# A top-k attention and gated feed-forward kernel: padded value tails, joined q and k tails, and a new order inside the slot

## The chip, the core and the metric

The kernel runs on one core of a Trainium2 chip. The metric is the time of one execution on the device in microseconds (us). PE is TensorE (PEld its weight loads), DVE is VectorE, ACT is ScalarE, POOL is GpSimd, SP is the queue that issues all DMAs of this kernel.

## What is computed

```python
batch, n_heads, seq, head_dim = (8, 8, 576, 64)          # q, k, v in float32
scores = scale * np.matmul(q, k.transpose(0, 1, 3, 2))
kth = np.partition(scores, -32, axis=-1)[..., -32:-31]
scores = np.where(scores >= kth, scores, -1e9)
scores = scores - np.max(scores, axis=-1, keepdims=True)
attn = np.exp(scores)
attn = attn / (np.sum(attn, axis=-1, keepdims=True) + 1e-09)
x = np.matmul(attn, v)                 # then (B,H,S,D) -> (B*S, H*D) = (4608, 512)
h = x @ w_in                           # w_in (512, 2048)
g = h * (1.0 / (1.0 + np.exp(-1.702 * h)))
out = g @ w_out                        # w_out (2048, 512)
```

## The kernel before

A row of 576 positions is four full tiles of 128 (`FULL` = 512) and a tail of 64 (`TAIL`). Heads are taken in pairs, four pairs a batch. The program is a list of 144 slots, 18 for each of the 8 batches: 16 slots of one query tile and one pair of heads, and two tail slots, in which the 64 last queries of two pairs share the 128 rows. Slot n works on several stages at once: the top-32 search on the scores of n (`topk`), the exponentials of n-1, the transposed weights and the product with v of n-2 (`turn`, `turn_tail`, `values`), the scores of n+1, and one quarter of a feed-forward tile (`hidden`: 16 matmuls of 128 columns into `ph`; `tanh`; `gate`; and, one slot later, `project`: 4 matmuls of 512 columns into `po`). A float32 matmul stands as two in the trace. A feed-forward tile is begun when the values of its four pairs are there; its fourth `project` is followed by `ob`, the copy of the result on ScalarE.

All engines run in the order in which the program is written. On TensorE a slot is: `turn`, `hidden`, `turn_tail`, `project`, `prepare` where there is one, `scores`, `values`. On ScalarE: the two copies of `turn`, the exponentials, the copy of `turn_tail`, tanh, the two preparatory operations on weights (`round_piece`), `ob`, the copies of `prepare`, the two copies of the scores, the copy of the values. VectorE does `topk` as a chain of 14 operations, with `divide` (two small ones; GpSimd then scales the weights `pr`) behind the ninth and `gate` behind the tenth.

`prepare` transposes one q or k tile pair: four full transposes and one of the 64 tail rows, each into a buffer of `ps_t`, which has two; `turn`, `turn_tail` and the output `o` of `values` use the same two. The tail of k is written at both ends of `k_t`, so that the scores of head 0 end with the tail keys and those of head 1 begin with them, and the two tails lie side by side in `pr`. The tail of v (`v_t`) is loaded twice, once for each half of the partitions, and `values` multiplies it from 64 partitions.

The weights, 32 pieces of 128x512, come in as 64-bit numbers and are rounded in the first slots, three a slot: `cut` and `sign` on VectorE (L137, L142), an addition on GpSimd (L146) and `normal` on VectorE (L149), with two temporaries from ScalarE (`more` L133, `size` L134) out of a pool of two buffers each.

Of the kernel before, what the change touches and what calls it, by code (L numbers as in the profile page):

```python
# [16 lines left out]
P = 128  # L17
# [9 lines left out]
def kernel(  # L27
# [44 lines left out]
    assert D == 64 and 2 * TAIL == P and C == NP * P and C == PIECE and HALF <= 512 and B % 2 == 0  # L72
# [5 lines left out]
    temps = pool("temps", 2)  # L78
# [78 lines left out]
    loaded = {}  # L157

    def load(name, b, hp):
        src = q if name == "q" else k  # L160
        t = loaded[name, b, hp] = loads.tile([P, NF + 1, 2, D], F32, name=f"{name}_l")
        for j in range(2):
            nc.sync.dma_start(
                t[:, 0:NF, j, :], src[b, 2 * hp + j, 0:FULL, :].rearrange("(t p) d -> p t d", p=P)
            )
        nc.sync.dma_start(
            t[0:TAIL, NF, :, :], src[b, 2 * hp : 2 * hp + 2, FULL:S, :].rearrange("h p d -> p h d")
        )

    def load_v(b, hp):  # L170
# [6 lines left out]
        tail = vals.tile([P, 2, D], F32, name="v_t")  # L177
        for i in range(2):
            nc.sync.dma_start(
                tail[i * TAIL : (i + 1) * TAIL, :, :],  # L180
                v[b, 2 * hp : 2 * hp + 2, FULL:S, :].rearrange("h p d -> p h d"),
            )
        vv[b, hp] = main, tail

    def prepare(name, b, hp):
# [5 lines left out]
        scale = SCALE if name == "q" else 1.0  # L191
        full = ps_t.tile([P, 512], F32, name="tp")
        for t in range(NF):
            nc.tensor.transpose(full[:, t * P : (t + 1) * P], src[:, t, :, :], ident[:])  # L194
        nc.scalar.mul(out=dst[:, before : before + FULL], in_=full[:], mul=scale)  # L195
# [15 lines left out]
    def scores(n):  # L211
        b, t, hps = slots[n]
        ps = [ps_s.tile([P, 2, 512], F32, name="s_ps") for _ in range(2)]
        if t < NF:
            parts = [(j, j, slice(0, P), slice(t * P, (t + 1) * P)) for j in range(2)]
        else:
            parts = [(i, j, slice(j * TAIL, (j + 1) * TAIL), slice(FULL, S)) for i in range(2) for j in range(2)]
        for c in range(2):
            for i, j, rows, cols in parts:
                on = slice(j * D, (j + 1) * D)  # L220
                nc.tensor.matmul(  # L221
                    ps[i][rows, c, 0:HALF],
                    lhsT=qT[b, hps[i]][on, cols],
                    rhs=kT[b, hps[i]][on, FIRST[i] + c * HALF : FIRST[i] + (c + 1) * HALF],
                )
# [56 lines left out]
    def turn(n):  # L282
        pr = st[n]["pr"]
        pt = st[n]["pt"] = ptp.tile([P, 2 * NF + 1, P], F32, name="pt")
        for i in range(2):
            tp = ps_t.tile([P, 512], F32, name="tp")
            for c in range(NF):
                nc.tensor.transpose(tp[:, c * P : (c + 1) * P], pr[:, MAIN[i] + c * P : MAIN[i] + (c + 1) * P], ident[:])  # L288
            nc.scalar.copy(out=pt[:, i * NF : (i + 1) * NF, :].rearrange("p c r -> p (c r)"), in_=tp[:])  # L289

    def turn_tail(n):

        tp = ps_t.tile([P, 512], F32, name="tp")
        nc.tensor.transpose(tp[:, 0:P], st[n]["pr"][:, FULL : FULL + P], ident[:])  # L294
        nc.scalar.copy(out=st[n]["pt"][:, 2 * NF, :], in_=tp[:, 0:P])
# [3 lines left out]
    def values(n):  # L299
# [3 lines left out]
        if t < NF:  # L303
            groups = [(0, [(j, slice(0, P), j) for j in range(2)])]
        else:
# [199 lines left out]
```

## Time and profile before

| | |
|---|---|
| Time, median of 3 runs | 1758.56 us (1758.18 to 1758.82) |
| Time of the profiled execution | 1759.57 us |
| Its span, first to last instruction | 1757.8 us |
| PE busy | 1640.2 us (93%) |
| DVE busy | 1582.3 us (90%) |
| ACT busy | 993.6 us (57%) |
| POOL busy | 599.1 us (34%) |
| Mean granted TensorE clock | 0.972 of full speed |

The busy share is a mean over two very different stretches: in the first 200 us the weights are rounded, and behind them all slots are alike. Each is read by itself.

### The profile page before, as it was taken

What the parts mean: (1) busy time and instruction counts of PE and PEld (TensorE: products, weight loads), DVE (VectorE), ACT (ScalarE), POOL (GpSimd) and SP (SyncE); (2) the same over time, 40 slices, a digit from 0 to 9 for tenths busy, and PEclk for the clock granted to TensorE, in tenths of its full rate; (3) what the DMA queues carried; (4) which work ended last, traced back from release to release, by engine and by line L of the source; (5) the groups of instructions that cost most, each with busy time, mean ns of one, the idle gap of its engine ahead of it and who ended that gap; (6) DMA issues with size and microseconds to landing.
All of it is one profiled execution on the core that took longest, in us unless ns stands there. A gap on an engine that the chain in (4) does not pass through costs nothing.

```text
span 1757.8 us, 31495 instructions
## 1 busy us (share of the span) xinstructions
PE 1640.2 (93%) x11856; PEld 1176.6 (67%) x11856; DVE 1582.3 (90%) x3408; ACT 993.6 (57%) x2149; POOL 599.1 (34%) x614
## 2 busy tenths in 40 slices
PE   2446899999999999999999999999999999999998
PEld 1225677667777777777777776777777777777776
DVE  5899998999899998999989998999989998999940
ACT  3456556656555555556565565555565565555530
POOL 2455432333333333333333333333323333333320
PEclk9668999999999999999999999999999999999999
DMA  7234001101000101010010100110010100000000
GB/s 198 77 112 123 12 16 36 37 6 28 21 22 21 35 21 35 14 35 22 20 29 21 35 21 21 29 35 22 19 30 21 35 21 20 22 7 7 7 7 13
DMA packets 129815, 57.61 MB, mean 33 GB/s; under 512 B 120960, under 2 KB 120960, under 8 KB 129664
## 3 DMA queue, kind: packets, MB, share of 16 engines
q1 hardware_dynamic: 129664, 55.60, 12.0%
q8 instruction: 94, 1.54, 0.4%
q14 instruction: 57, 0.47, 0.1%
HBM read 46.14 MB, written 9.44 MB: 32 GB/s over the span
## 4 chain that ended last, share of the span: by engine, by line
PE 87%; DVE 8%; ACT 1%; issue 1%; POOL 1%; SPq 1%; DMA 0%; POOLq 0%; DVEq 0%
PE ph L353 28%; PE po L391 27%; PE o L318 11%; PE s_ps L221 10%; PE tp L288 8%; DVE top L237 3%; DVE left L240 2%; PE tp L194 2%; PE tp L294 1%; DVE win L142 1%; ACT k_t L195 1%; DVE win L137 1%; DVE wout L142 1%; POOL pr L280 0%; PE tp L197 0%
## 5 line engine op out<-in xcount | busy, mean ns | idle before, releaser
L280 POOL TENSOR_SCALAR pr<-pr,rden 128x576 f32<-128x576 f32 x288 | 493.4, 1725 | 924.7 <-DVE rden L277 801.1
L237 DVE MAX8 top<-left 128x8 f32<-128x576 f32 x864 | 623.0, 747 | 0.0
L391 PE MATMUL po<-wout,gT 128*128 128x512 f32 x1152 | 518.0, 592 | 0.0
L353 PE MATMUL ph<-xT,win 128*128 128x128 f32 x4096 | 483.9, 277 | 0.0
L353 PEld LDWEIGHTS ph<-xT,win 128*128 128x128 f32 x4096 | 473.4, 194 | 0.5 <-issue 0.5
L240 DVE MATCH_REPLACE8 left<-top,left 128x576 f32<-128x576 f32 x576 | 423.4, 743 | 0.0
L391 PEld LDWEIGHTS po<-wout,gT 128*128 128x128 f32 x1152 | 207.8, 190 | 207.1 <-issue 206.8
L228 ACT COPY sc<-s_ps 128x576 f32<-128x576 f32 x288 | 169.8, 642 | 304.5 <-PE s_ps L221 304.5
L237 DVE MAX8 top<-sc 128x8 f32<-128x576 f32 x288 | 204.5, 751 | 104.9 <-ACT sc L228 101.4
L288 PE MATMUL tp<-ident,pr 128*128 128x128 f32 x1152 | 172.7, 289 | 53.8 <-POOL pr L280 37.8
L267 ACT ACTIVATE pr<-sc,low 128x576 f32<-128x576 f32 x288 | 219.3, 764 | 0.0
L240 DVE MATCH_REPLACE8 left<-top,sc 128x576 f32<-128x576 f32 x288 | 211.9, 743 | 0.0
L265 ACT ACTIVATE sc<-sc,cut 128x576 f32<-128x576 f32 x288 | 207.5, 771 | 0.0
L221 PE MATMUL s_ps<-k_t,q_t 64*128 64x288 f32 (+1 forms) x1280 | 202.8, 436 | 1.6 <-ACT k_t L195 1.6
L289 ACT COPY pt<-tp 128x512 f32<-128x512 f32 x288 | 157.5, 586 | 52.8 <-PE tp L288 52.6
L288 PEld LDWEIGHTS tp<-ident,pr 128*128 128x128 f32 x1152 | 124.4, 144 | 91.5 <-POOL pr L280 41.1
L221 PEld LDWEIGHTS s_ps<-k_t,q_t 64*128 64x128 f32 (+1 forms) x1280 | 114.6, 183 | 93.5 <-issue 71.1
L318 PEld LDWEIGHTS o<-pt,v_l 128*64 128x64 f32 x2560 | 129.2, 138 | 59.9 <-issue 41.2
L318 PE MATMUL o<-pt,v_l 128*64 128x128 f32 (+1 forms) x2560 | 165.0, 272 | 0.0
L377 DVE SCALAR_TENSOR_TENSOR gT<-th,ph 128x512 f32<-128x512 f32 x144 | 96.5, 670 | 49.5 <-ACT th L370 49.5
L370 ACT ACTIVATE th<-ph 128x512 f32<-128x512 f32 x144 | 86.8, 603 | 32.2 <-PE ph L353 32.2
L396 ACT ACTIVATE ob<-po 128x512 f32<-128x512 f32 x36 | 21.5, 598 | 97.6 <-PE po L391 97.6
(45 smaller groups left out, 905.7 us busy)
## 6 DMA issues: line engine op xcount, KB each, us to landing
v_l<-in_v_dram SPq DMA_DIRECT2D x64, 128.0 KB, 2.5
q_l<-in_q_dram SPq DMA_DIRECT2D x64, 128.0 KB, 2.5
k_l<-in_k_dram SPq DMA_DIRECT2D x64, 128.0 KB, 2.5
raw<-in_moe_w_in_dram SPq DMA_DIRECT2D x16, 512.0 KB, 4.8
raw<-in_moe_w_out_dram SPq DMA_DIRECT2D x16, 512.0 KB, 3.8
out_dram<-ob SPq DMA_DIRECT2D x32, 256.0 KB, 2.1
v_t<-in_v_dram SPq DMA_DIRECT2D x64, 32.0 KB, 2.2
q_l<-in_q_dram SPq DMA_DIRECT2D x32, 32.0 KB, 2.3
```

The lines of the kernel that those rows point to most:

```text
L221: nc.tensor.matmul(ps[i][rows, c, 0:HALF], lhsT=qT[b, hps[i]][on, cols], rhs=kT[b, hps[i]][on, FIRST[i] + c * HALF : FIRST[i] + (c + 1) * ...
L228: nc.scalar.copy(out=sc[:, i, :].rearrange("p (c k) -> p c k", c=2), in_=ps[i][:, :, 0:HALF])
L237: nc.vector.max(top[:, i, 8 * r : 8 * r + 8], (left if r else sc)[:, i, :])
L240: nc.vector.match_replace(left[:, i, :], top[:, i, 8 * r : 8 * r + 8], (left if r else sc)[:, i, :], LOWEST)
L265: nc.scalar.activation(sc[:, i, :], sc[:, i, :], AF.Prelu, bias=cut[:, i : i + 1], alpha=HUGE)
L267: nc.scalar.activation(pr[:, i * S : (i + 1) * S], sc[:, i, :], AF.Exp, bias=low[:, i : i + 1], accum_out=den[:, i : i + 1],)
L280: nc.gpsimd.tensor_scalar(on, on, rden[:, i : i + 1], None, op0=ALU.mult)
L288: nc.tensor.transpose(tp[:, c * P : (c + 1) * P], pr[:, MAIN[i] + c * P : MAIN[i] + (c + 1) * P], ident[:])
L289: nc.scalar.copy(out=pt[:, i * NF : (i + 1) * NF, :].rearrange("p c r -> p (c r)"), in_=tp[:])
L318: nc.tensor.matmul(dst, lhsT=lhsT, rhs=rhs, start=(c == 0), stop=(c == NF))
L353: nc.tensor.matmul(ph[:, i, :], lhsT=win[:, c, f * P : (f + 1) * P], rhs=xT[:, c, :], start=(c == 0), stop=(c == CC - 1),)
L391: nc.tensor.matmul(po[:], lhsT=gT[:, i, :], rhs=wout[:, f, :], start=(f == 0), stop=(f == FC - 1))
```

## The change

Six edits, made together. (1) The tail of v lies in one of six constant tiles `v_e`, zero but for head 0's tail in the upper left and head 1's in the lower right quarter, and `values` multiplies it from all 128 partitions, as it does the full tiles. (2) The tails of q and k of a pair come into one tile `ends` and are turned by one transpose, in the `prepare` of k. (3) In tail slots the two score tiles are now the two heads, and the rows the two pairs (before, the other way round); the four quarter-size products go in the order (0,0), (1,1), (0,1), (1,0) of row half and column half. (4) The order inside the slot: `scores` and `values` come before `project`, `prepare` before them, the exponentials before the copies of `turn`; `divide` stands behind the sixth operation of the chain and `gate` behind the last; `hidden` starts as soon as a tile is ready (slot 6, before slot 7). (5) Three buffers for each temporary of the weights, whose ScalarE operations now stand at the end of the slot ahead. (6) Two pieces are loaded and rounded ahead of the first chain, and the loads of q and k stand ahead of those of v.

```diff
-    temps = pool("temps", 2)
+    temps = pool("temps", 3)
...
+    v_ends = [const.tile([P, 2, D], F32, name=f"v_e{i}") for i in range(6)]
+    for t in v_ends:
+        nc.gpsimd.memset(t[:], 0.0)
...
-        tail = vals.tile([P, 2, D], F32, name="v_t")
-        for i in range(2):
-            nc.sync.dma_start(
-                tail[i * TAIL : (i + 1) * TAIL, :, :],
-                v[b, 2 * hp : 2 * hp + 2, FULL:S, :].rearrange("h p d -> p h d"),
-            )
+        tail = v_ends[(b * NP + hp) % len(v_ends)]
+        for j in range(2):
+            nc.sync.dma_start(tail[j * TAIL : (j + 1) * TAIL, j, :], v[b, 2 * hp + j, FULL:S, :])
...
-        tail = ps_t.tile([P, 512], F32, name="tp")
-        nc.tensor.transpose(tail[:, 0:TAIL], src[0:TAIL, NF, :, :], ident[0:TAIL, 0:TAIL])
-        for left_at in (0, before + FULL) if before else (FULL,):
-            nc.scalar.mul(out=dst[:, left_at : left_at + TAIL], in_=tail[:, 0:TAIL], mul=scale)
+        if name == "k":
+            ends = ps_t.tile([P, 512], F32, name="tp")
+            nc.tensor.transpose(ends[:, 0:P], loaded.pop(("ends", b, hp))[:], ident[:])
+            nc.scalar.mul(out=qT[b, hp][:, FULL:S], in_=ends[:, 0:TAIL], mul=SCALE)
+            for to in (0, before + FULL):
+                nc.scalar.copy(out=dst[:, to : to + TAIL], in_=ends[:, TAIL:P])
...
-            parts = [(j, j, slice(0, P), slice(t * P, (t + 1) * P)) for j in range(2)]
+            parts = [(i, 0, slice(0, P), slice(t * P, (t + 1) * P)) for i in range(2)]
         else:
-            parts = [(i, j, slice(j * TAIL, (j + 1) * TAIL), slice(FULL, S)) for i in range(2) for j in range(2)]
+            parts = [(i, p, slice(p * TAIL, (p + 1) * TAIL), slice(FULL, S)) for i, p in ((0, 0), (1, 1), (0, 1), (1, 0))]
...
-                    if c < NF:
-                        lhsT, rhs = main[:, c, j, :], pt[:, tile_ * NF + c, cols]
-                    else:
-                        on = slice(half * TAIL, (half + 1) * TAIL)
-                        lhsT, rhs = tail[on, j, :], pt[on, 2 * NF, cols]
-                    nc.tensor.matmul(dst, lhsT=lhsT, rhs=rhs, start=(c == 0), stop=(c == NF))
+                    nc.tensor.matmul(
+                        o[j * D : (j + 1) * D, 0 : cols.stop - cols.start],
+                        lhsT=main[:, c, j, :] if c < NF else tail[:, j, :],
+                        rhs=pt[:, j * NF + c if c < NF else 2 * NF, cols],
...
-        if 0 <= n - 2 < N:
-            turn(n - 2)
-        if n >= NPIECE // RATE - NG + 1:
-            hidden()
         if 0 <= n - 1 < N:
             bounds(n - 1)
             exponentials(n - 1)
         if 0 <= n - 2 < N:
-            turn_tail(n - 2)
-        tanh()
-        rounding = [round_piece(x) for x in by_slot[n]] if 0 <= n < len(by_slot) else []
-        project()
+            turn_main(n - 2)
+        hidden()
+        if 0 <= n - 2 < N:
+            turn_ends(n - 2)
         for fn, args in todo:
             if fn is prepare:
                 fn(*args)
+        tanh()
         if n + 1 < N:
             scores(n + 1)
         if 0 <= n - 2 < N:
             values(n - 2)
+        project()
+        if n == -1:
+            begin_rounding(-1)
+        begin_rounding(n + 1)
...
-            if i == 8 and 0 <= n - 1 < N:
+            if i == 5 and 0 <= n - 1 < N:
                 divide(n - 1)
-            if i == 9:
-                gate()
...
+        gate()
```

On TensorE an ordinary slot, from the transposes of `pr` on, stood thus before:

```order
L288 MATMUL tp<-ident,pr 128x128 x8
L353 MATMUL ph<-xT,win 128x128 x16
L294 MATMUL tp<-ident,pr 128x128
L391 MATMUL po<-wout,gT 128x512 x4
L221 MATMUL s_ps<-k_t,q_t 128x288 x4
L318 MATMUL o<-pt,v_l 64x128 x8
L318 MATMUL o<-pt,v_t 64x128 x2
```

The same slot of the changed kernel, where `v_e_126` is one of the six tail tiles:

```order
L297 MATMUL tp<-ident,pr 128x128 x8
L361 MATMUL ph<-xT,win 128x128 x16
L297 MATMUL tp<-ident,pr 128x128
L229 MATMUL s_ps<-k_t,q_t 128x288 x4
L320 MATMUL o<-pt,v_l 64x128 x8
L320 MATMUL o<-pt,v_e_126 64x128 x2
L399 MATMUL po<-wout,gT 128x512 x4
```

The four wide matmuls of `project` moved from ahead of the scores to the end of the slot, and the transposes of the next slot now follow them.

On ScalarE the part of a slot around `ob`, the copy of a finished feed-forward tile, stood thus before (from tanh to the exponentials of the next slot):

```order
L370 ACTIVATE th<-ph 128x512
L396 ACTIVATE ob<-po 128x512
L228 COPY sc<-s_ps 128x576 x2
L324 COPY xT<-o 128x128
L289 COPY pt<-tp 128x512 x2
L265 ACTIVATE sc<-sc,cut 128x576 x2
L267 ACTIVATE pr,den<-sc,low 128x576 x2
```

And in the changed kernel:

```order
L378 ACTIVATE th<-ph 128x512
L236 COPY sc<-s_ps 128x576 x2
L332 COPY xT<-o 128x128
L404 ACTIVATE ob<-po 128x512
L273 ACTIVATE sc<-sc,cut 128x576 x2
L275 ACTIVATE pr,den<-sc,low 128x576 x2
L298 COPY pt<-tp 128x512 x2
```

`ob` moved behind the copies of scores and values, directly ahead of the exponentials, and the two copies of `turn` moved behind these.

On VectorE the program began with the first chain:

```order
L237 MAX top<-sc 128x8 x2
L137 TENSOR_SCALAR win<-raw 128x512
L240 MATCH_REPLACE left<-top,sc 128x576
L142 SCALAR_TENSOR_TENSOR win<-raw,win 128x512
L240 MATCH_REPLACE left<-top,sc 128x576
```

It now begins with two whole pieces of weights:

```order
L137 TENSOR_SCALAR win<-raw 128x512
L142 SCALAR_TENSOR_TENSOR win<-raw,win 128x512
L137 TENSOR_SCALAR win<-raw 128x512
L142 SCALAR_TENSOR_TENSOR win<-raw,win 128x512
L149 SCALAR_TENSOR_TENSOR win<-size,win 128x512 x2
L245 MAX top<-sc 128x8 x2
```

All six operations on the first two pieces, the two `normal` included, stand ahead of the first search.

## Rows read from the trace of the kernel before

**Rows 1.** Windows: length; busy PE, PEld, DVE, ACT, POOL; clock, DMA share, GB/s

```profile
200.00:1700.00 1500.00, 1489.19 (x10974) 1069.91 (x10973) 1404.75 (x3060) 884.36 (x1926) 509.55 (x534) 1.00 0.09 23
```

**Rows 2.** Waits of PE and of DVE from 200 to 1700: us, times, longest

```profile
PE tp L194 <- ACT k_t L195: 6.9, 14, 0.5
...
DVE top L237 <- ACT sc L228: 75.9, 116, 2.5
```

**Rows 3.** Timeline of PE, an ordinary slot: start us, us, what

```profile
600.93 0.43 PE L318 MATMUL o<-pt,v_t 64*64 64x128 f32 x4
601.29 1.16 PE L288 MATMUL tp<-ident,pr 128*128 128x128 f32 x8
602.29 3.74 PE L353 MATMUL ph<-xT,win 128*128 128x128 f32 x32
...
605.97 3.60 PE L391 MATMUL po<-wout,gT 128*128 128x512 f32 x8
609.50 1.24 PE L221 MATMUL s_ps<-k_t,q_t 64*128 64x288 f32 x8
610.67 1.09 PE L318 MATMUL o<-pt,v_l 128*64 128x128 f32 x16
611.69 0.43 PE L318 MATMUL o<-pt,v_t 64*64 64x128 f32 x4
```

**Rows 4.** Timeline of PE, tail slots: values of one, scores of another

```profile
704.71 0.69 PE L318 MATMUL o<-pt,v_l 128*64 128x64 f32 x16
705.33 0.33 PE L318 MATMUL o<-pt,v_t 64*64 64x64 f32 x4
...
706.47 1.10 PE L288 MATMUL tp<-ident,pr 128*128 128x128 f32 x8
...
855.62 2.16 PE L221 MATMUL s_ps<-k_t,q_t 64*64 64x288 f32 x16
857.71 1.09 PE L318 MATMUL o<-pt,v_l 128*64 128x128 f32 x16
```

**Rows 5.** Timeline of DVE: the starts of four chains that waited for nothing

```profile
89.45 1.41 DVE L237 MAX8 top<-sc 128x8 f32<-128x576 f32 x2
105.16 1.41 DVE L237 MAX8 top<-sc 128x8 f32<-128x576 f32 x2
...
209.48 1.40 DVE L237 MAX8 top<-sc 128x8 f32<-128x576 f32 x2
219.99 1.41 DVE L237 MAX8 top<-sc 128x8 f32<-128x576 f32 x2
```

**Rows 6.** Timeline of ACT: the exponentials of a slot, first and last, and one `ob`

```profile
602.97 1.44 ACT L265 ACTIVATE sc<-sc,cut 128x576 f32<-128x576 f32 x2
...
605.74 0.19 ACT L267 ACTIVATION_READ_ACCUMULATOR pr<-sc,low 128x1 f32 x1
...
620.37 0.60 ACT L396 ACTIVATE ob<-po 128x512 f32<-128x512 f32 x1 [2.67 <-PE po L391]
```

**Rows 7.** Timeline of the start: DMA issues on SP, two ACT operations on weights

```profile
0.71 1.00 SPq L173 DMA_DIRECT2D v_l<-in_v_dram  x2
...
3.21 1.15 SPq L163 DMA_DIRECT2D q_l<-in_q_dram  x2
...
10.56 1.54 SPq L115 DMA_DIRECT2D raw<-in_moe_w_in_dram  x3
...
15.81 0.67 ACT L133 ACTIVATE more<-raw 128x512 int32<-128x512 uint32 x1 [2.30 <-DMA raw<-in_moe_w_in_dram]
...
28.35 0.66 ACT L134 ACTIVATE size<-raw 128x512 f32<-128x512 f32 x1 [8.66 <-DVE win L149]
```

**Rows 8.** Waits of DVE from 0 to 90, and GpSimd's addition (lines view)

```profile
DVE top L237 <- ACT sc L228: 25.5, 4, 13.0
DVE win L137 <- DMA raw<-in_moe_w_in_dram: 1.4, 1, 1.4
...
L146 POOL TENSOR_TENSOR win<-win,more 128x512 int32<-128x512 int32 x16 | 20.5, 1294 | 58.9 <-DVE win L142 33.1 <-ACT more L133 25.9
```

More of the change, by code (lines that the diff above doesn't have):

```diff
@@ L71 @@
     SCALE = 1.0 / float(D) ** 0.5
[L72 removed]
+    assert D == 64 and 2 * TAIL == P and C == NP * P and C == PIECE and B % 2 == 0
     assert TOPK == 32 and NP == 4 and NF == 4 and NG == 4 and CC == 4
@@ L280, in divide, with turn, turn_main, turn_ends @@
             nc.gpsimd.tensor_scalar(on, on, rden[:, i : i + 1], None, op0=ALU.mult)
-    def turn(n):
+    def turn(n, first, cols, blocks):
         pr = st[n]["pr"]
-        pt = st[n]["pt"] = ptp.tile([P, 2 * NF + 1, P], F32, name="pt")
-        for i in range(2):
[L286 to L295, printed above, removed]
+        if first == 0:
+            st[n]["pt"] = ptp.tile([P, 2 * NF + 1, P], F32, name="pt")
+        to = st[n]["pt"][:, first : first + blocks, :].rearrange("p c r -> p (c r)")
+        tp = ps_t.tile([P, 512], F32, name="tp")
+        for c in range(blocks):
+            nc.tensor.transpose(tp[:, c * P : (c + 1) * P], pr[:, cols + c * P : cols + (c + 1) * P], ident[:])
+        nc.scalar.copy(out=to, in_=tp[:, 0 : blocks * P])
+    def turn_main(n):
+        for i in range(2):
+            turn(n, i * NF, MAIN[i], NF)
+    def turn_ends(n):
+        turn(n, 2 * NF, FULL, 1)
     xts = {}
@@ L302, in values @@
         outs = []
[L303 to L308 removed]
+        for p in range(2 if t == NF else 1):
+            cols = slice(p * TAIL, (p + 1) * TAIL) if t == NF else slice(0, P)
+            main, tail = vv[b, hps[p]]
             o = ps_t.tile([P, 512], F32, name="o", tag="tp")
             for c in range(NF + 1):
[L311 to L319 removed]
+                for j in range(2):
+                    nc.tensor.matmul(
+                        o[j * D : (j + 1) * D, 0 : cols.stop - cols.start],
+                        lhsT=main[:, c, j, :] if c < NF else tail[:, j, :],
+                        rhs=pt[:, j * NF + c if c < NF else 2 * NF, cols],
+                        start=(c == 0),
+                        stop=(c == NF),
+                    )
+            outs.append((o, hps[p]))
         for o, hp in outs:
@@ L410 @@
     VALUES = (-8, -7, 1, 2)
+    by_slot = {-1: [0, 1]}
+    for x in range(2, NPIECE):
+        by_slot.setdefault((x - 2) // 3, []).append(x)
     for hp in range(NP):
-        at(hp - 1, load_v, 0, hp)
         for name in "qk":
@@ L415 @@
             at(hp - 1, prepare, name, 0, hp)
+        if hp == 0:
+            for x in by_slot[-1]:
+                at(-1, load_piece, x)
+    for hp in range(NP):
+        at(hp - 1, load_v, 0, hp)
+    for n in range(NPIECE // 3):
+        for x in by_slot[n]:
+            at(n - 1, load_piece, x)
     for b in range(1, B):
@@ L421, with begin_rounding @@
             at(b * PER + VALUES[hp], load_v, b, hp)
-    RATE = 3
-    by_slot = [list(range(i, min(i + RATE, NPIECE))) for i in range(0, NPIECE, RATE)]
-    for n, some in enumerate(by_slot):
-        for x in some:
-            at(n - 1, load_piece, x)
+    rounding, last = {}, []
+    def begin_rounding(n):
+        rounding[n] = [round_piece(x) for x in by_slot.get(n, [])]
     def slot(n):
@@ L451, in slot @@
             values(n - 2)
+        project()
+        if n == -1:
+            begin_rounding(-1)
+        begin_rounding(n + 1)
         chain = topk(n) if 0 <= n < N else [lambda: None] * 14
-        first = [op for ops, _ in rounding for op in ops]
-        last = [op for _, op in rounding]
+        some = rounding.pop(n)
+        first = [op for ops, _ in some for op in ops]
+        last.extend(op for _, op in some)
         for i, op in enumerate(chain):
             op()
-            if i == 8 and 0 <= n - 1 < N:
+            if i == 5 and 0 <= n - 1 < N:
                 divide(n - 1)
-            if i == 9:
-                gate()
             if i and first:
                 first.pop(0)()
-            elif last and i > 11:
+            elif last and i > 8:
                 last.pop(0)()
-        for op in first + last:
-            op()
+        while first:
+            first.pop(0)()
+        while last and n >= 0:
+            last.pop(0)()
+        gate()
     with tc.manual_schedule():
```

27 lines of the change are left out of this document (12 added, 15 removed).

## The prediction

> **What bounds the kernel now.** I read the windows view first, then the waits, then one slot engine by engine. From 200 to 1700 us TensorE is busy 1489 of 1500 us at the full clock (granted 1.00, the level of 2.4 GHz) and VectorE 1405 [rows 1]. Busy time of overlapping matmuls proves little, so the waits decide: in those 1500 us VectorE waits 75.9 us in 116 places for the copied scores, that is, for what TensorE makes, while the largest wait of TensorE is 6.9 us in 14 places [rows 2]. TensorE sets the pace. An ordinary slot is 10.76 us of it (600.93 to 611.69) [rows 3]. VectorE is close behind: a chain that waits for nothing takes 10.51 us (209.48 to 219.99) [rows 5]. So there are only 0.25 us to take from an ordinary slot before VectorE is the bound there; slots with a `prepare` and tail slots are longer on TensorE and leave more.
>
> Before 200 us VectorE is the bound: it does the weights beside the searches (15.7 us a chain with three pieces [rows 5]). Of its first 90 us it waits 25.5 us for scores, 13.0 of them at the very start, and 1.4 us for the first piece [rows 8]. The repeated ones come from ScalarE: `size` of the third piece of a slot stands 8.66 us waiting for VectorE's `normal`, which frees a temporary [rows 7], and behind it in ScalarE's order stand the copies that the next scores need.
>
> **The change, part by part.**
>
> *Start: 13.6 us less.* VectorE's work there stays the same, so only its waits count, 26.9 us now. Afterwards q is issued at 0.71 in place of 3.21 and the first weights at about 4.5 in place of 10.56 [rows 7]. The first piece took 5.25 us from issue to use (10.56 to 15.81), so it is there at about 9.8 and the second some 2 us later. The scores, two us earlier than now, are copied by 11.6 (estimate). Then ScalarE makes four temporaries at 0.67 us [rows 7]; `more` of the second piece ends at 11.6 + 3 x 0.67 = 13.6, the addition on GpSimd takes 1.3 [rows 8], the last `normal` about 0.7: the first search starts at some 15.5 us, later than today's 13.0, but with two pieces done. A piece costs VectorE (15.7 - 9.9) / 3 = 1.9 us, where 9.9 is a chain of 10.51 less the gate's 0.6 (estimate), which no slot has yet [rows 5]. So 15.5 - 3.9 = 11.6 us of waiting are left, and I add 1.7 for the third piece, whose load now stands behind those of the second pair and of v. The waits for later scores go: with three buffers no `size` waits inside its own chain, and it stands behind the copies of the scores. 26.9 - 13.3 = 13.6. Bounds: 16 if the pieces come on time, 5 if ScalarE is held at each slot's end by a late load.
>
> *Ordinary slots: 0.21 us less, 110 times, 23.1 us.* `values` runs two matmuls at once: 16 of 128 columns take 1.02 us (610.67 to 611.69), where `hidden` and the transpose behind it take (605.97 - 602.29) / 33 = 0.11 for each one of the same width [rows 3]; so a pair is 0.11, and 8 pairs 0.89. The other 0.13 is the change to another shape of the array (64*64 behind 128*64). The tail's two pairs take 0.36 to 0.37 (600.93 to 601.29), again 0.22 of work and 0.15 of change. As two more pairs of the same shape they cost 0.22: 0.15 less. `turn`, eight transposes, takes 1.00 in place of 8 x 0.11 = 0.88 behind such a change [rows 3]; it now follows `project`, of its own shape, and gains 0.12; `project` takes over the change, of which I give back half, 0.06. Moving `project` adds no work. The new slot is 10.55, still above 10.51. I count slots 14 to 143 without the four around slot 24 (below): 110 ordinary and 16 tail slots. Bounds: 0.15 a slot (16.5 us) and 0.25 (27.5 us, VectorE's pace).
>
> *Values of tail slots: 0.54 us less, 16 times, 8.6 us.* Two groups now take 1.76 us (704.71 to 706.47), each 0.62 for eight pairs of 64 columns and 0.26 for the tail [rows 4]. Afterwards it is one run of 20 pairs: 0.62 and 12 more pairs at half of 0.11, 1.28 in all, and the 0.06 at `turn` as above.
>
> *Scores of tail slots: 0.97 us less, 16 times, 15.5 us, or nothing.* Sixteen matmuls of 288 columns on a quarter of the array take 2.09 us (855.62 to 857.71); one alone is 288/128 x 0.11 = 0.25, so two run at once, in eight steps of about 0.24 [rows 4]. The old order used only the quarters (0,0) and (1,1), in turn. The new one names all four in a row. That two matmuls share the rows and differ in columns is shown by `values` (128*64), and that they share the columns and differ in rows by the ordinary scores (64*128, eight in 1.17 us) [rows 3]. That both hold together no row shows. I take four at once, four steps for eight, 4 x 0.24 = 0.97 less; the other bound is zero.
>
> By the Trainium skill, "TensorEngine Tiling (Array Packing)", Key Properties, the 64x64 mode has four tiles that load and multiply independently, which by itself would give the same halving; the same list says that a change of mode drains the engine, and the 0.13 to 0.15 us at each change agree with that. Its Gotcha 1 says that different row tiles cannot use one PSUM bank at a time; the old pairs (0,0), (1,1) wrote one bank from two row halves and still ran together, so here the trace does not bear it out.
>
> *Joined ends of q and k: nothing.* A transpose of 64 rows goes and one of 128 takes the place of two; but the old ones had the shape of the scores behind them and paid no change of their own. Saved at most 0.1 us a pair on 28 pairs; the copies on ScalarE stay five. In the two slots a batch with two `prepare`, TensorE's wait for a buffer (0.5 us, 14 times [rows 2]) stays.
>
> *`hidden` one slot earlier: 1.5 us with the last two slots.* It moves 7.1 us of TensorE (32 x 0.11 and 609.50 - 605.97 = 3.53 [rows 3]) to slots where VectorE is the bound. But the tile that would follow is ready only at the end of slot 23 (its values are those of slot 21), so slots 22 and 23 both go without, and VectorE sets 9.9 to 10.5 us there: the gain is one gate and a few handovers.
>
> *The order on ScalarE and VectorE: nothing, and here is the cover.* New slot, us from its start: `turn` to 0.9, `hidden` to 4.45, ends 4.6, scores 4.65 to 5.8, values to 7.05, `project` to 10.55. Scores are copied at 5.9 to 7.1, the chain of VectorE starts at 6.65 as the first copy ends. ScalarE then copies the values (7.5) and does the exponentials, 2.96 us (602.97 to 605.93) [rows 6], until 10.4; `divide` stands four searches and two replacements into the chain, about 4.1 us, at 10.75: in time. Every fourth slot `ob` stands ahead of them and waits for the end of `project` (today it costs 2.67 us of idle ScalarE, with scores queued behind it [rows 6]): 10.75 to 11.25, so the exponentials end at 14.2 and VectorE stands 3.45 us in `divide`. Behind that wait are the rest of the chain, its gate and the next chain. Who waits for those? `hidden` two slots on needs `ph`, freed by the gate: the gate of a chain in time ends 3.9 us before the slot that it must precede, and `hidden` starts 0.9 into it, so VectorE can be 4.8 us late before TensorE feels it. The transposed weights need GpSimd's scaling, with over 6 us to spare. The copies of `turn` end 0.2 us before `turn_ends` needs their buffer. So 3.45 us late stays covered, by 1.35; and it doesn't add up, since the next `ob` delays to the same offset and a chain in between gains 0.04 (ordinary) to 0.5 us (`prepare`).
>
> **The sum.** 13.6 + 23.1 + 8.6 + 15.5 + 1.5 = 62.3 us from the profiled execution, span 1757.8, time 1759.57: 1697.3. The median of the runs is 1.0 below that time: 1696.3, and I say 1697.
>
> **The rivals.**
>
> *Quarters still in pairs.* Nothing in the trace has three at once. Then 15.5 us stay: 1712.
>
> *The wait in `divide` reaches TensorE in part.* The margin of 1.35 us and the 0.2 us at `turn_ends` are small, and a slot with `ob` and a `prepare` of k has three more small copies ahead of tanh. With 1 us lost at each of the 36 `ob`, or VectorE bound in ordinary slots, the time is about 1733.
>
> *Slower.* One mechanism: ScalarE, held by `ob` until `project` is done, releases the chain 3.45 us late, and if no cover holds, every `ob` costs that on TensorE: 36 x 3.45 = 124 us, 1821. It decides from 62.3 / 36 = 1.7 us lost at each `ob`. Against it stands the count of slots between the late gate and its user.
>
> *The start gives nothing.* The two early `normal` hold VectorE until 15.5 us; if loads come late as well, the first term is 0 and the time 1710.
>
> **How the numbers follow.** Chances: the forecast 0.50, pairs 0.25, partly lost 0.14, no gain at the start 0.05, slower or no change 0.06. The forecast alone spans 1688 to 1706 (its bounds of the start and of the ordinary slots). For 8 in 10 the range takes in the pairs with a part of the loss: 1688 to 1729. Within 0.2% (3.5 us, about what a measurement here can tell) I put 0.02, slower 0.04, faster 0.94.
>
> **What would show it.** Tail scores: a group of 16 in about 1.1 us, or still 2.1. Values: one group of 20 in about 1.25, and an ordinary slot of 10.55. Start: the first search at 15 to 16, and no wait of 4 us for scores behind it. VectorE: its waits move from scores to `divide` on ScalarE's `pr`, up to 3.5 us, some 36 times, and TensorE shows no new wait. The prediction is wrong if TensorE waits for `gate`, for `pt` copies or for GpSimd's `pr` in the steady slots, or if the slot stays at 10.7.

## The result and the profile after

The changed kernel takes 1710.56 us (median of four runs, 1709.99 to 1711.98) where the kernel before took 1758.37 on the same chip: a ratio of 0.9729 (95% interval 0.9712 to 0.9746). That is faster, inside the range, and 13.6 us above the forecast of 1697. It lies outside the 1688 to 1706 that the prediction gave the forecast alone: the range holds it because it was widened for the rivals. One execution of all those below, the profiled one of tail_pairs, ran at a granted clock of 0.715 in the mean and took 2172.1 us, so its trace is not read for times, and the median of tail_pairs would be 1710.34 without it. The intervals of the ratios reach some 3 us to each side, so differences of that size are read from the traces as well. The profiled execution took 1710.55 us with a span of 1708.6, so 49.2 us of span are gone where the sum had said 62.3. TensorE is busy 94% of the span and VectorE 93%.

The windows view of the changed kernel, from 200 to 1660 us (columns as in [rows 1]):

```profile
200.00:1660.00 1460.00, 1445.75 (x10933) 1068.08 (x10932) 1389.19 (x3041) 872.34 (x1917) 506.18 (x532) 1.00 0.09 23
```

The waits of TensorE, and then those of VectorE, of the changed kernel in the same stretch:

```profile
PE tp L199 <- ACT k_t L201: 6.6, 14, 0.6
PE tp L297 <- ACT pt L298: 4.9, 3, 3.3
```

```profile
DVE some L283 <- ACT pr L275: 45.6, 32, 3.5
DVE gT L385 <- ACT th L378: 14.5, 9, 8.8
```

TensorE still sets the pace of the steady part. VectorE's 75.9 us of waiting for scores [rows 2] are gone. In their place VectorE waits 32 times in `divide`, 1.4 us in the mean and 3.5 at the longest. TensorE now waits 4.9 us in three places for the copies of `turn` (it had waited 0.2 once) and 1.9 us once for the gate. All four waits lie between 315 and 343 us; we come back to them under the experiment with `ob`.

An ordinary slot in the timeline of TensorE, changed kernel (the counterpart of [rows 3]):

```profile
572.11 1.04 PE L297 MATMUL tp<-ident,pr 128*128 128x128 f32 x8
572.98 3.74 PE L361 MATMUL ph<-xT,win 128*128 128x128 f32 x32
576.55 0.27 PE L297 MATMUL tp<-ident,pr 128*128 128x128 f32 x1
576.75 1.24 PE L229 MATMUL s_ps<-k_t,q_t 64*128 64x288 f32 x8
577.92 1.09 PE L320 MATMUL o<-pt,v_l 128*64 128x128 f32 x16
578.85 0.39 PE L320 MATMUL o<-pt,v_e 128*64 128x128 f32 x4
579.17 3.70 PE L399 MATMUL po<-wout,gT 128*128 128x512 f32 x8
582.71 1.04 PE L297 MATMUL tp<-ident,pr 128*128 128x128 f32 x8
```

From start to start the slot takes 10.60 us (572.11 to 582.71); it was 10.76. What each block takes is read as the difference of its start and the next. `turn` has 0.87 (it was 1.00). The values have 1.25, 0.93 and 0.32 for the tail (they were 1.02 and 0.36). The lone transpose ahead of the scores has 0.20 (it was 0.11). `project` has 3.54, as before: it gained a change of shape at its start and lost the one at its end, and that one is now the 0.09 behind the transpose. That a change was in the old 3.53 shows where a `prepare` of q, which has the shape of `project`, came next: there `project` took 3.43 in the kernel before (818.81 to 822.24).

Scores of a tail slot, and values of another, in the same timeline (the counterpart of [rows 4]):

```profile
630.88 1.20 PE L229 MATMUL s_ps<-k_t,q_t 64*64 64x288 f32 x16
632.01 1.09 PE L320 MATMUL o<-pt,v_l 128*64 128x128 f32 x16
...
667.91 0.69 PE L320 MATMUL o<-pt,v_l 128*64 128x64 f32 x16
...
669.23 3.70 PE L399 MATMUL po<-wout,gT 128*128 128x512 f32 x8
```

The sixteen quarters of the scores take 1.13 us (630.88 to 632.01) where they took 2.09: four run at once. The values of a tail slot take 1.32 (667.91 to 669.23) where they took 1.76.

The start of the changed kernel in the timeline of VectorE: the first search, and two neighbouring chains behind it (the counterpart of [rows 5]):

```profile
15.26 1.41 DVE L245 MAX8 top<-sc 128x8 f32<-128x576 f32 x2
...
63.83 1.39 DVE L245 MAX8 top<-sc 128x8 f32<-128x576 f32 x2
...
80.04 0.73 DVE L245 MAX8 top<-sc 128x8 f32<-128x576 f32 x1
```

The waits of VectorE in the first 90 us, changed kernel (the counterpart of [rows 8]):

```profile
DVE win L137 <- DMA raw<-in_moe_w_in_dram: 9.3, 3, 8.7
DVE win L149 <- POOL win L146: 1.8, 1, 1.8
```

The first search starts at 15.26 (forecast 15.5), and VectorE's waits fell from 26.9 to 11.1 us (forecast 13.3). But a chain with three pieces of weights now takes 16.2 us (63.83 to 80.04), where it took 15.7 [rows 5]. The chain of the twelfth slot starts at 190.22 where it had started at 198.97: 8.75 us earlier, though 15.8 us of waiting are gone. So VectorE's own work in this stretch has grown by 7.0 us, which the prediction had put at nothing; 0.6 of it is one more gate, since `hidden` starts a slot earlier.

Where it grew shows in the lines view of VectorE from 0 to 190 us, with shapes apart, changed kernel (busy us, mean ns of one):

```profile
L149 DVE SCALAR_TENSOR_TENSOR win<-size,win 128x512 f32<-128x512 f32 x16 | 13.2, 832 | 1.8 <-POOL win L146 1.8
L149 DVE SCALAR_TENSOR_TENSOR wout<-size,wout 128x512 f32<-128x512 f32 x16 | 12.6, 788 | 0.0
...
L137 DVE TENSOR_SCALAR wout<-raw 128x512 uint32<-128x512 uint32 x16 | 9.7, 605 | 0.0
L283 DVE TENSOR_SCALAR some<-den 128x2 f32<-128x2 f32 x10 | 7.7, 775 | 0.0
```

In the same view of the kernel before, the means of these four were 675, 675, 501 and 515 ns. Times their counts that is 2.5 + 1.8 + 1.7 + 2.6 = 8.6 us more; `sign` (L142) gave back 2.2 (747 and 743 ns, now 676 and 675, 32 of them). One chain shows what they meet. First VectorE's timeline, then GpSimd's, changed kernel:

```profile
35.10 1.04 DVE L137 TENSOR_SCALAR win<-raw 128x512 uint32<-128x512 uint32 x1
...
37.99 0.84 DVE L283 TENSOR_SCALAR some<-den 128x2 f32<-128x2 f32 x1
...
38.95 0.41 DVE L137 TENSOR_SCALAR win<-raw 128x512 uint32<-128x512 uint32 x1
...
40.00 0.68 DVE L142 SCALAR_TENSOR_TENSOR win<-raw,win 128x512 uint32<-128x512 uint32 x1
...
42.66 0.68 DVE L149 SCALAR_TENSOR_TENSOR win<-size,win 128x512 f32<-128x512 f32 x1
...
43.98 1.04 DVE L149 SCALAR_TENSOR_TENSOR win<-size,win 128x512 f32<-128x512 f32 x1
```

```profile
34.59 1.26 POOL L146 TENSOR_TENSOR win<-win,more 128x512 int32<-128x512 int32 x1 [2.64 <-DVE win L142]
37.54 1.26 POOL L146 TENSOR_TENSOR win<-win,more 128x512 int32<-128x512 int32 x1 [1.69 <-DVE win L142]
39.20 3.44 POOL L288 TENSOR_SCALAR pr<-pr,rden 128x576 f32<-128x576 f32 x2 [0.40 <-DVE rden L285]
42.62 1.85 POOL L146 TENSOR_TENSOR win<-win,more 128x512 int32<-128x512 int32 x1
```

The same `cut` takes 0.41 us alone (38.95) and 1.04 when it starts half a microsecond into an addition on GpSimd (35.10). `some`, four values a partition, ends at 38.83, just as the addition of 37.54 ends (38.80). Where the two start together (42.62 and 42.66), `normal` keeps its 0.68 and the addition takes 1.85. So the one that comes later is held by the other. How long can be read from the twelve kernels that have the addition and whose traces are read. An addition that is not held itself takes 1.26 to 1.28 us; an operation of the rounding, or `some`, that starts within it takes as long as if it had started 1.14 to 1.17 us after the addition's start (162 records). Each of the two operations of GpSimd's scaling takes 1.72; one that starts in its first 0.6 us takes as long as if it had started 0.60 to 0.63 us after (57 records), and one that starts later keeps its own time: the `sign` at 40.00, 0.80 us into the scaling of 39.20, took its usual 0.68. By the Trainium skill, "SBUF — State Buffer", section "SBUF: two separate sides", VectorE and GpSimd share one port pair that is locked for a whole instruction, by a VectorE operation with two SBUF inputs or in its two-port mode, or by one of GpSimd; the rows of the addition come near that. Those of GpSimd's scaling do not: it holds for 0.6 us of its 1.72.

### The profile page after: what moved, and what is told of

Read it like the earlier page. It is cut to its first block, busy times and chain, and to the rows that moved or that the text cites. A ratio compares the mean times of both kernels' runs of the same rounds, so it can differ in the third digit from the quotient of the medians.

```text
span 1708.6 us, 31456 instructions
## 1 busy us (share of the span) xinstructions
PE 1604.8 (94%) x11824; PEld 1183.7 (69%) x11824; DVE 1581.2 (93%) x3408; ACT 989.5 (58%) x2149; POOL 595.1 (35%) x620
## 4 chain that ended last, share of the span: by engine, by line
PE 87%; DVE 11%; SPq 1%; ACT 1%; issue 0%; DMA 0%; DVEq 0%
PE po L399 29%; PE ph L361 29%; PE o L320 10%; PE s_ps L229 9%; PE tp L297 8%; DVE top L245 4%; DVE left L248 3%; PE tp L199 2%; DVE wout L149 1%; DVE wout L142 1%; DVE win L149 1%; DVE win L137 1%; ACT k_t L201 0%; DVE wout L137 0%; DVE win L142 0%
## 5 line engine op out<-in xcount | busy, mean ns | idle before, releaser
L245 DVE MAX8 top<-left 128x8 f32<-128x576 f32 x864 | 610.1, 746 | 0.0
L399 PE MATMUL po<-wout,gT 128*128 128x512 f32 x1152 | 532.0, 605 | 0.0
L361 PE MATMUL ph<-xT,win 128*128 128x128 f32 x4096 | 489.5, 279 | 18.4 <-DVE gT L385 18.4
L361 PEld LDWEIGHTS ph<-xT,win 128*128 128x128 f32 x4096 | 478.3, 196 | 20.7 <-DVE gT L385 19.7
L298 ACT COPY pt<-tp 128x512 f32<-128x512 f32 (+1 forms) x432 | 188.7, 470 | 227.6 <-PE tp L297 227.2
L297 PEld LDWEIGHTS tp<-ident,pr 128*128 128x128 f32 x1296 | 157.3, 143 | 129.4 <-issue 62.1
L297 PE MATMUL tp<-ident,pr 128*128 128x128 f32 x1296 | 195.1, 278 | 50.6 <-ACT pt L298 37.7
L229 PE MATMUL s_ps<-k_t,q_t 64*128 64x288 f32 (+1 forms) x1280 | 187.4, 440 | 0.9 <-ACT k_t L201 0.9
L264 POOL TENSOR_SCALAR cut<-top 128x2 f32<-128x2 f32 x144 | 31.9, 222 | 304.5 <-DVE top L245 304.5
L229 PEld LDWEIGHTS s_ps<-k_t,q_t 64*128 64x128 f32 (+1 forms) x1280 | 102.1, 181 | 41.0 <-issue 20.6
```

Of the source, the lines that this page charges most:

```text
L229: nc.tensor.matmul(ps[i][rows, c, 0:HALF], lhsT=qT[b, hps[p]][on, cols], rhs=kT[b, hps[p]][on, FIRST[i] + c * HALF : FIRST[i] + (c + 1) * ...
L245: nc.vector.max(top[:, i, 8 * r : 8 * r + 8], (left if r else sc)[:, i, :])
L297: nc.tensor.transpose(tp[:, c * P : (c + 1) * P], pr[:, cols + c * P : cols + (c + 1) * P], ident[:])
L298: nc.scalar.copy(out=to, in_=tp[:, 0 : blocks * P])
L361: nc.tensor.matmul(ph[:, i, :], lhsT=win[:, c, f * P : (f + 1) * P], rhs=xT[:, c, :], start=(c == 0), stop=(c == CC - 1),)
L399: nc.tensor.matmul(po[:], lhsT=gT[:, i, :], rhs=wout[:, f, :], start=(f == 0), stop=(f == FC - 1))
```

## The experiments

Ratios are to the kernel before, on the same chip. The edits are to the changed kernel, where nothing else is said.

**v_half: the tail of v on half the rows again, all else as changed.**

```diff
-lhsT=main[:, c, j, :] if c < NF else tail[:, j, :]
+lhsT=main[:, c, j, :] if c < NF else tail[j * TAIL : (j + 1) * TAIL, j, :]
...
-rhs=pt[:, 2 * NF, cols]
+rhs=pt[j * TAIL : (j + 1) * TAIL, 2 * NF, cols]
```

> The changed kernel, but values multiplies the tail of v from 64 partitions again (the zero halves are left out of the product, the result is the same). If the gain of an ordinary slot comes from the missing change of shape: the slot goes from 10.60 to about 10.75 us, two groups of tail values from 1.32 back to 1.76, together 117 x 0.15 + 16 x 0.44 = 24 us more, about 1735. Rival, that the order of project made the gain: within 3 us of 1711.

1733.86 us, ratio 0.986 (0.9845 to 0.9874): 23.3 us slower than the changed kernel. The timeline of TensorE, an ordinary slot with a `prepare` of this kernel:

```profile
605.97 1.09 PE L320 MATMUL o<-pt,v_l 128*64 128x128 f32 x16
606.99 0.44 PE L320 MATMUL o<-pt,v_e 64*64 64x128 f32 x4
607.36 3.70 PE L399 MATMUL po<-wout,gT 128*128 128x512 f32 x8
```

The tail is the shape 64*64 once more, and the values take 1.39 in place of 1.25. The ordinary slot is 10.75 us, nearly that of before. So without the padding the other moves on TensorE give nothing in an ordinary slot: the gain there is the change of shape that is no longer made.

**tail_only: the kernel before, with nothing but the new assignment of the tail scores.** The edit is to the kernel before: the assignment of the tail scores, the score tiles and operands that go with it, and in `values`

```diff
+parts = [(i, p, slice(p * TAIL, (p + 1) * TAIL), slice(FULL, S)) for i, p in ((0, 0), (1, 1), (0, 1), (1, 0))]
...
+groups = [(p, [(j, slice(p * TAIL, (p + 1) * TAIL), j) for j in range(2)]) for p in range(2)]
```

> The kernel before with one edit: in tail slots rows are pairs and score tiles are heads, so that all four quarters of the array are used; the tail of v is still multiplied from 64 partitions. If the tail scores alone give what the prediction put on them: the group of 16 goes from 2.09 to 1.13 us in 16 slots, 15.4 us less, 1743. Rival, that VectorE takes the gain back in those slots or that the four need the rest of the change: 1750 to 1758.

1741.6 us, ratio 0.9906 (0.9891 to 0.9921): 17.1 us less than the kernel before. In the timeline of its TensorE the group is as in the changed kernel (1.13 us, 646.93 to 648.06):

```profile
646.93 1.20 PE L221 MATMUL s_ps<-k_t,q_t 64*64 64x288 f32 x16
648.06 1.09 PE L318 MATMUL o<-pt,v_l 128*64 128x128 f32 x16
```

This term stands by itself, and needs nothing else of the change. In the trace the 16 slots give 15.4 us, 0.96 each. Another 1.6 lie in one `hidden`, which took 5.20 us at a granted clock of 0.67 in the kernel before (from 355.49) and took 3.57 at 1.00 here (from 363.23), and 1.1 lie ahead of slot 11; these two are not the tail scores'.

**tail_pairs: only two different quarters next to one another in the tail scores.**

```diff
+work = [(c, parts[x]) for first in (0, 2) for c in range(2) for x in (first, first + 1)]
```

> The changed kernel, but the tail scores use the quarters (0,0) and (1,1) for both column parts first and then (0,1) and (1,0), so that only two different quarters stand next to each other. If four ran at once: the group of 16 goes from 1.13 to 2.1 us in 16 slots, 15 us more, about 1726. Rival, that the order inside the group doesn't matter: 1711.

1710.44 us, ratio 0.9723 (0.9707 to 0.9739): no difference. **tail_order: the four quarters in another order.**

```diff
-((0, 0), (1, 1), (0, 1), (1, 0))
+((0, 0), (0, 1), (1, 0), (1, 1))
```

> The changed kernel with the four quarters in the order (0,0), (0,1), (1,0), (1,1), in which neighbours share the row half or nothing. If any four different quarters run at once: 1711, the group of 16 still 1.13 us. Rival, that neighbours must differ in both halves: pairs, up to 15 us more, 1718 to 1726.

1710.32 us, ratio 0.9721 (0.9705 to 0.9738): no difference; the group takes 1.13 us here too (239.66 to 240.79). Both say the same. What halves the time is that all four quarters are used; in what order the instructions name them does not count. My reading of the old order, that naming two in turn is what held it to pairs, was right only in that it named no more than two.

**ends_apart: the tails of q and k turned separately again.** Each `prepare` has its own tile and its own transpose of 64 rows:

```diff
+nc.tensor.transpose(ends[:, 0:TAIL], src[0:TAIL, :, :], ident[0:TAIL, 0:TAIL])
```

> The changed kernel with the tails of q and k in tiles of their own and turned apart from 64 rows, as before. Theory after the result: the joined transpose costs, since a 64-row transpose has the shape of the scores behind it and hides its change there; slots with a prepare of k should lose 0.18 us, slots with one of q gain 0.05: 28 x 0.13 = 3.6 us less, about 1707. Rival, the step of the prediction: no difference, or up to 3 us more, 1711 to 1714.

1710.56 us, ratio 0.9729 (0.9714 to 0.9743): no difference. After the result I had come to think that the joined ends cost some 4 us; that fell. The timeline of TensorE, a `prepare` of q in this kernel:

```profile
600.59 0.60 PE L197 MATMUL tp<-ident,q_l 128*128 128x128 f32 x4
601.12 0.27 PE L202 MATMUL tp<-ident,ends_q 64*128 64x64 f32 x1
601.13 1.29 PE L225 MATMUL s_ps<-k_t,q_t 64*128 64x288 f32 x8
```

A transpose of 64 rows is nearly free ahead of the scores (0.01 us to their start), since it has their shape; the joined one, behind the `prepare` of k, costs 0.25 (607.11 to 607.36 in the kernel with `ob` late, below). The slot with a `prepare` of k is 11.09 us apart and 11.28 joined. It comes back where the separate way pays more: the slot with a `prepare` of q is 11.10 apart and 11.04 joined, and 11.20 apart against 11.00 joined where the scores behind it are of a tail. At the start the separate ends cost 2.4 us more in the profiled execution, which was the longest of its four (1713.64). By the medians the sum is nothing, as the prediction had it.

**ob_late: the copy `ob` behind the exponentials and behind the copies of `turn`.** `project` leaves its copy and its store to a function that is called later in the next slot:

```diff
             turn_main(n - 2)
+        finish()
```

> The changed kernel, but the copy ob of a finished tile stands in the next slot behind the exponentials and the copies of turn. If TensorE never felt VectorE's wait in divide: that wait (45.6 us in 32 places from 200 to 1660) goes to nearly nothing and the time stays at 1711 within 2 us. Rival, that the wait reached TensorE in part: 5 to 30 us less.

1707.79 us, ratio 0.9714 (0.9698 to 0.9731): 2.8 us better. Its waits of VectorE from 200 to 1660 us:

```profile
DVE gT L385 <- ACT th L378: 44.4, 37, 8.8
DVE some L283 <- ACT pr L275: 2.7, 1, 2.7
```

The waits in `divide` are gone (45.6 to 2.7 us). VectorE waits at its gate instead (14.5 us before this edit, 44.4 now), and an ordinary slot still takes 10.60. So these waits are time that VectorE has to spare, and cost TensorE nothing in the steady part: the cover that the prediction named holds. The gain is in one place, between the `hidden` of slot 21 and that of slot 24, where VectorE sets the pace for lack of feed-forward: 27.40 us became 24.33, and the slot behind it 11.92 in place of 11.31. There the wait in `divide` reached TensorE: its waits at `tp` for `pt` lie there, 0.8 us before 315.64 and 3.25 before 326.14 in the changed kernel, 0.2 and 1.4 with `ob` late. Behind the longer one TensorE's clock was low as well. The changed kernel from there, in the windows view and in the timeline of TensorE:

```profile
326.40:330.10 3.70, 3.70 (x25) 2.69 (x26) 3.67 (x12) 1.55 (x4) 3.23 (x2) 0.54 0.69 156
```

```profile
326.40 2.07 PE L229 MATMUL s_ps<-k_t,q_t 64*128 64x288 f32 x8
328.40 1.89 PE L320 MATMUL o<-pt,v_l 128*64 128x128 f32 x16
```

At a granted clock of 0.54, near the lower level of 1.2 GHz, scores and values took 2.00 and 1.72 us (to 330.12). With `ob` late they took 1.17 and 0.93 (324.10 to 326.20) at a clock of 1.00. So 1.6 us of TensorE's time there is the clock behind the wait, and not the wait itself.

**no_add: GpSimd's addition left out.** The kernel leaves out the low words of the weights, so their last bits are missing from the product.

```diff
-nc.gpsimd.tensor_tensor(out=whole, in0=whole, in1=more[:], op=ALU.add)
```

> The changed kernel without GpSimd's addition in the rounding of the weights (their low words are left out). If VectorE's small operations are stretched in the first 180 us because they run beside that addition: chains with three pieces go from 16.2 to about 14.5 us, the wait of 1.8 and a second of the first two normal go too, 15 to 19 us less, 1692 to 1696. Rival, that late loads or ScalarE hold the start: 3 us less at most, 1708.

1692.65 us, ratio 0.9628 (0.9613 to 0.9642): 17.9 us less than the changed kernel. A chain with three pieces takes 14.52 us. The lines view of its VectorE from 20 to 170 us:

```profile
L149 DVE SCALAR_TENSOR_TENSOR wout<-size,wout 128x512 f32<-128x512 f32 x16 | 10.9, 678 | 0.0
L149 DVE SCALAR_TENSOR_TENSOR win<-size,win 128x512 f32<-128x512 f32 x14 | 9.5, 679 | 0.0
...
L137 DVE TENSOR_SCALAR wout<-raw 128x512 uint32<-128x512 uint32 x16 | 6.6, 410 | 0.0
```

Every group is at the duration that its operation has alone. VectorE itself does the same operations as in the changed kernel: so the addition, by standing beside them, is what lengthens the chain.

**pack: `cut` and `sign` of one piece next to one another.**

```diff
-if i and first: first.pop(0)()
+if i % 2 and first: first.pop(0)(); first.pop(0)()
```

> The changed kernel with cut and sign of a piece side by side behind the second, fourth and sixth operation of the chain, so that the addition runs beside two searches or replacements and not beside the next cut or divide. Nothing else moves. If the collisions cost, about 1.3 us a chain in 9 chains go: 1699 to 1703. Rival, that the order on VectorE doesn't matter: 1711.

1706.12 us, ratio 0.9704 (0.9689 to 0.9718): 4.4 us better, about half of the least that I had expected. The chain is 15.92 us. The first two additions then run beside the searches. But the third `sign` starts 0.16 us into GpSimd's scaling, and the third addition waits behind the scaling and meets the first `normal`. The timeline of its VectorE, and then of its GpSimd:

```profile
69.16 1.12 DVE L142 SCALAR_TENSOR_TENSOR win<-raw,win 128x512 uint32<-128x512 uint32 x1
...
72.99 1.22 DVE L149 SCALAR_TENSOR_TENSOR wout<-size,wout 128x512 f32<-128x512 f32 x1
```

```profile
69.00 3.43 POOL L288 TENSOR_SCALAR pr<-pr,rden 128x576 f32<-128x576 f32 x2 [0.42 <-PE s_ps L229]
72.39 1.27 POOL L146 TENSOR_TENSOR win<-win,more 128x512 int32<-128x512 int32 x1
```

**pack_div8: besides, `divide` behind the ninth operation in slots with weights**, so that the scaling stands behind the additions.

```diff
-if i == 5 and 0 <= n - 1 < N:
+if i == (8 if some else 5) and 0 <= n - 1 < N:
```

> Cut and sign side by side, and divide behind the ninth operation of the chain in the slots with weights, so that the third addition on GpSimd does not wait for the scaling of the weights and runs beside two replacements. If only the additions stretch VectorE's small operations: a chain with three pieces goes from 15.9 to 14.7 us, 9 to 11 us less than with cut and sign alone, 1695 to 1698. Rival, that the scaling stretches the three normal as well: no gain, 1704 to 1708.

1702.51 us, ratio 0.9683 (0.9668 to 0.9697): 3.6 us better still, some third of what I had expected, and a chain of 15.55. `cut` and `sign` now have nearly their own durations (425 and 693 ns), `normal` has not. The timeline of its VectorE, and then of its GpSimd:

```profile
72.15 0.91 DVE L149 SCALAR_TENSOR_TENSOR wout<-size,wout 128x512 f32<-128x512 f32 x1
...
73.71 1.04 DVE L149 SCALAR_TENSOR_TENSOR win<-size,win 128x512 f32<-128x512 f32 x1
...
75.40 0.68 DVE L149 SCALAR_TENSOR_TENSOR win<-size,win 128x512 f32<-128x512 f32 x1
```

```profile
71.77 3.42 POOL L288 TENSOR_SCALAR pr<-pr,rden 128x576 f32<-128x576 f32 x2 [1.17 <-DVE rden L285]
```

The first starts 0.38 us into the scaling's first operation, the second 0.24 us into its second (which starts at 73.47), and each is held until 0.61 us after that start; the one behind the scaling is not held. In the kernel before, the `normal` at 102.71 stood 0.79 us into the second operation of a scaling (101.92) and took 0.67. So it is not the kind of operation that decides, but how soon after the start of GpSimd's it comes.

**round_here: the rounding's ScalarE operations in their own slot, ahead of the scores, with three buffers.**

```diff
-begin_rounding(n + 1)
...
+if n >= 0: begin_rounding(n)
```

> The changed kernel with the two ScalarE operations of each piece of weights in the slot of the piece and ahead of the copies of prepare and scores, where they stood before; three buffers and the two early pieces stay. If their place in ScalarE's order took the waits of 4.17 us away: VectorE waits for scores again in the first slots, 4 to 13 us more, 1715 to 1724. Rival, that the third buffer alone does it: 1711.

1714.94 us, ratio 0.9754 (0.9738 to 0.977): 4.4 us slower, at the lower end. In the timeline of its VectorE a chain takes 17.1 us (searches start at 65.40 and 82.52) in place of 16.2.

But VectorE does not wait for scores once in its first 195 us here, so the way that the expectation named is not the one. What grew, in the lines view of that stretch, are the `normal` (946 and 905 ns in the mean, 832 and 788 in the changed kernel) and their waits for the addition (4.4 us, 1.8 in the changed kernel). So three buffers and the two early pieces end the waits for scores without the new place, and the place in ScalarE's order counts, 4.4 us, by which operations of VectorE and GpSimd then meet. How the rest divides between the third buffer and the early pieces was not tried.

**best: ends_apart, pack and ob_late together.**

> Three edits of the other runs together: tails of q and k apart, cut and sign side by side, ob behind the exponentials. If they add up: 3.6 and 8 to 12 us less than the changed kernel, 1695 to 1700. Rival, that they hide behind each other: 1704 to 1708.

1703.71 us, ratio 0.9691 (0.9676 to 0.9705): 6.9 us below the changed kernel, near the sum of what the three gave alone (0, 4.4 and 2.8), and short of the forecast because two of them were. **best2: pack_div8 and ob_late, joined ends.**

> The same with ob behind the exponentials. If the start and the stretch around slot 23 are independent: 2.5 to 3 us less than without, 1692 to 1696. Rival, that they are not: no difference between the two.

1700.87 us (1700.41 to 1701.4), ratio 0.9672 (0.9657 to 0.9686): the best version here, 57.8 us below the kernel before and 9.7 below the changed kernel. By the medians `ob` gave 1.6 us on top of pack_div8, whose four runs lie 3.0 us apart; by the spans of the two traces (1701.7 and 1698.9) it gave 2.8, as alone.

## Why the prediction was right and wrong

The direction, the bound and the order of the terms were right; two sizes were too large, and one step failed. The measured column is the difference of the two traces, taken where the `hidden` of a slot starts: 6.60 us at slot 11 (198.78 and 192.18), 7.14 at slot 13, 10.77 at slot 21, 12.72 at slot 25, 48.24 at slot 143 and 49.2 at the end.

| step | predicted | measured |
|---|---|---|
| start | 13.6 | 6.6, and 0.5 up to slot 13 |
| ordinary slots, 110 | 23.1 | 17.4 |
| values of tail slots, 16 | 8.6 | 5.3 |
| scores of tail slots, 16 | 15.5 | 16.5 |
| slots 22 to 25 and the end | 1.5 | 2.9 |
| sum | 62.3 | 49.2 |

The slots 14 to 143 without the four around slot 24 gave (10.77 - 7.14) + (48.24 - 12.72) = 39.15. Of these the tail scores are 16 x 1.03 (slots of 11.68 and 12.32 became 10.56 and 11.00; less the 0.165 and 0.22 that a slot of their kind gains anyway). The tail values are 16 x 0.33 (12.91 to 12.45 and 11.56 to 11.36). The rest, 17.4, is the ordinary slots', 0.158 each.

**Start: the step that failed is "VectorE's work there stays the same, so only its waits count".** The waits fell even more than forecast, by 15.8 against 13.6, and the first search came at 15.26 as worked out. But VectorE's work took 7.0 us more, some 0.5 in each chain with three pieces. Most of it comes with an edit that I had priced at nothing: `divide` moved from the ninth operation of a chain to the sixth. GpSimd's scaling comes with it and now stands between the second and the third addition (39.20 ahead of 42.62 above). So `some` falls into the second addition (2.6 us in all) and the second `normal` of a chain into the third (nine times 0.36, 3.2 us). In the kernel before, the three additions were through when `normal` came, which took 0.67 throughout, and `some` met at most the third: it took 0.14 us in four of the ten chains up to 198 us (44.51 and 64.26 are two) and 0.35 to 1.11 in the others. Of the rest, 1.1 us is one of the two early `normal`, held by an addition ahead of the first search (the two take 2.34 us from 12.99), 0.6 is the gate, and `cut` and `sign` together gave 0.4 back. That the additions hold VectorE is shown by taking them away (17.9 us, which includes what they already cost before). That the place of `divide` is part of it is shown by pack_div8, where the old place, in these slots alone, gave 3.6 us; the changed kernel with the old place and nothing else was not run. The rival with no gain at the start did not come in full: 6.6 of the 13.6 us were left. The trace of before held the warning: its `cut` took 643 and 501 ns in the mean, where one alone takes 410, beside an addition of 1294 ns [rows 8] on an engine that I took for independent.

**Ordinary slots: the mis-sized term is the change of shape at `project`, "of which I give back half, 0.06".** It pays the whole, 0.09 to 0.10: that is the difference of the transpose ahead of the scores (0.11 to 0.20), since `project`'s own 3.53 had held one change already (3.43 without). The values gained 0.13 for the 0.15 forecast, `turn` 0.13 for 0.12. Slots with a `prepare` of k alone gained nothing (11.26 to 11.28), and they were counted among the 110.

**Tail values: 0.54 forecast, 0.33 measured.** The run of values itself went from 1.76 to 1.32, near the 1.28 forecast. What was left out stands around it: both slots of a batch that have such values also have a `prepare` of k, and in one of the two its joined ends cost 0.25 (677.84 to 678.10, where the old ones cost 0.01); and `project` pays its change in both.

**Tail scores: right.** Four quarters run at once; the rival with pairs (1712) did not come, though the total came near it for other reasons. The total alone would have pointed to that rival; the group of 1.13 us excludes it, and so does tail_only.

**Joined ends: nothing, right**, as a sum of gains and losses of up to 0.2 us a slot. **The order on ScalarE and VectorE: right in the steady slots**, where 45.6 us of waits in `divide` moved TensorE by nothing (10.60 with and without them); they were 1.4 us in the mean, not the 3.45 that was reckoned for each, so the full margin was not put to the test. It was too good at slots 21 to 25: there no cover was reckoned, TensorE waited for the copies of `turn` and the gate, and the wait in `divide` cost 2.8 us, part of it by the lower clock behind it, taken from a gain that was larger than forecast all the same.

## What to carry to other kernels

When an operation of VectorE or GpSimd is moved, look at which of the other's instructions it will run beside: an operation whose mean is longer than its single record when nothing runs beside it is held by someone, and a new order decides who is held next. Here half a microsecond decides: what starts in the first 0.6 us of a scaling is held, what starts later is not. On TensorE count the changes of array shape around a whole slot before and after, and charge each one in full; padding a short operand with zeros can be cheaper than a shape of its own (here 1.25 us of values in place of 1.38). A wait that is covered in the steady part still costs in the few slots where its engine is the bound, so check cover by stretches.

## What was not expected of the hardware

- Sixteen matmuls on quarters of the array take 1.13 us with all four in use, in either order whose group was read, against 2.09 with two.
- An operation of VectorE that starts within GpSimd's two-input addition is held until 1.14 to 1.17 us after the addition's start: `cut` takes 1.04 for 0.41 us, `some` 0.84 for 0.15. The other way round the addition took 1.85 for 1.26. The searches kept 0.74 to 0.75 us throughout.
- GpSimd's scaling holds VectorE only in the first 0.6 us of each of its operations of 1.72: `sign` took 1.12 when it started 0.16 us into one, `normal` 0.91 at 0.38, and `sign` 0.68 at 0.80.
- After waits of 0.8 and 3.3 us TensorE's granted clock was 0.54 for 3.7 us, and scores and values took 3.72 us for 2.10; the wait alone understates what it costs.
